# Two transposed loads in place of one for x tiles 2 and 3, and one load in place of two for the value weights

## Chip, cores, metric

One NeuronCore of a Trainium2 chip. The metric is the time of one execution on the device in microseconds (us), the median of several. The span in a profile (first to last instruction) is about 1.7 us shorter than that time. There is one core, so no die to compare with.

## The reference, cut

The result mixes two blocks over the same x of 2048 rows by 512 columns: `g * a + (1 - g) * b`, where g is a sigmoid gate of each row. Block a is linear attention with 32 heads; block b is a gated MLP.

```python
x = A_x
g = _sigmoid((x * gate_w).sum(-1, keepdims=True))
# block a
qkv = x @ wqkv                     # split into q, k, v; k and q go through w_phi and softmax
...
# block b
z = gelu(x @ w_in)
z1 = z[..., :Fh]
z2 = layernorm(z[..., Fh:])
gg = einsum('ts,bsf->btf', w_sp, z2) + b_sp
b = (z1 * gg) @ w_out
```

What matters here is the very beginning: z2 and z1 are computed for one row tile of 128 rows after another, and each needs x transposed, its half of `w_in`, and for z2 one extra column with the gate weights.

## The kernel before, the parts concerned

Tiles 0 and 1 of x are loaded plainly and transposed on TensorE; all others are transposed by their load, and the sync engine issues all of these. The loads, in the order of the program (`nc.sync` and `nc.scalar` name the engine that issues):

```python
    nc.sync.dma_start(out=xs[:, 0, :], in_=x2[0:P, :])
    nc.scalar.dma_start(out=xs[:, 1, :], in_=x2[P:2 * P, :])
    load_z2w(nc.sync, 0)
    load_z2w(nc.scalar, 1)
    load_z2w(nc.sync, 2)
    nc.scalar.dma_start(out=gaterow[0:NDT, :], in_=gate_w.rearrange("(dt p) -> dt p", p=P))
    load_z2w(nc.sync, 3)
    # ... (cut)
    def x_dma_T(i, n=1):
        nc.sync.dma_start_transpose(out=xT[:, :, i * P:(i + n) * P], in_=x2[i * P:(i + n) * P, :])

    x_dma_T(2, 2)
    for h in range(2):
        nc.sync.dma_start(
            out=w_z1[:, 2 * h:2 * h + 2, :], in_=w_in_v[:, 2 * h:2 * h + 2, 0:FH])
    for i in range(4, 8):
        x_dma_T(i)
    # ... (cut: x tiles 8 to 15, bias, folded weights)
    for h in range(2):
        nc.sync.dma_start(
            out=wv_sb[:, 2 * h:2 * h + 2, :],
            in_=A_wqkv[h * 2 * P:(h + 1) * 2 * P, 2 * D:3 * D].rearrange("(dt p) n -> p dt n", p=P),
        )
    # ... (cut: four transposed loads of w_sp)
```

TensorE works in this order (six warm-up matmuls and one short one first):

```python
        z2_first_two()          # tiles 0 and 1, by parts as the z2 weights arrive;
                                # in it, gate_T() turns the gate weights into a column of w_z2
        z2_tile(2)
        z2_tile(3)
        for c in range(NCH):
            # ... z2 of the chunk's tiles (c > 0), then z1 of its four tiles
```

Each z2 or z1 tile is eight matmuls. The first z1 tile needs the first half of the z1 weights at its first matmul, and the second half at its fifth.

The softmax here doesn't subtract the row's maximum and nothing guards it: scores larger than these inputs give would overflow.

## Time and profile before

| | before |
|---|---|
| time, median (3 runs) | 206.92 us (206.57 to 206.94) |
| span of the profiled run (a fourth run, 206.23 us) | 204.5 us |
| TensorE busy | 98% |
| z2 of tile 2 starts (first matmul) | 7.27 us |
| second z1 tile starts | 10.79 us |
| end of TensorE's work after that | 190.9 us later |

In the timeline, a row gives start, length, engine, source line, operation and count; in brackets stands how long that engine was idle before, and what ended it. PE is a matmul, PEld the load of its weights, SPq an issue on the sync engine. The landing views give kilobytes and the time from issue to landing. The lines themselves are in the prediction below. One more line of before's timeline, the five matmuls from 5.17 us in the first two tiles:

```profile
5.17 0.89 PE L191 MATMUL zp<-w_z,xT 128*128 128x344 bf16 x5
```

Five matmuls in 0.89 us: four steps of 0.145 to 0.147 us and 0.31 us for the last one.

### The profile page before, as it was taken

What the parts mean: (1) busy time and instruction counts of PE and PEld (TensorE: products, weight loads), DVE (VectorE), ACT (ScalarE), POOL (GpSimd) and SP (SyncE); (2) the same over time, 40 slices, a digit from 0 to 9 for tenths busy, and PEclk for the clock granted to TensorE, in tenths of its full rate; (3) what the DMA queues carried; (4) which work ended last, traced back from release to release, by engine and by line L of the source; (5) the groups of instructions that cost most, each with busy time, mean ns of one, the idle gap of its engine ahead of it and who ended that gap; (6) DMA issues with size and microseconds to landing.
All of it is one profiled execution on the core that took longest, in us unless ns stands there. A gap on an engine that the chain in (4) does not pass through costs nothing.

```text
span 204.5 us, 3996 instructions
## 1 busy us (share of the span) xinstructions
PE 200.6 (98%) x1557; PEld 119.5 (58%) x1557; DVE 130.5 (64%) x283; ACT 74.6 (36%) x122; POOL 45.8 (22%) x76
## 2 busy tenths in 40 slices
PE   8999999999999999999999999999999999999994
PEld 3566666655665555656565666555555555665642
DVE  4567484837977587979797788555566645633332
ACT  3466678796222333332424042222251136002303
POOL 3020202021523325334242442222204220200000
PEclk9999999999999999999999999999999999999999
DMA  5998599999997017950422229763567458552943
GB/s 188 247 209 151 117 277 209 241 194 234 207 290 168 3 38 148 317 97 15 77 47 46 51 38 114 142 126 62 108 161 79 90 112 184 61 96 51 141 80 104
DMA packets 89931, 27.22 MB, mean 133 GB/s; under 512 B 84184, under 2 KB 89912, under 8 KB 89912
## 3 DMA queue, kind: packets, MB, share of 16 engines
q1 hardware_dynamic: 87744, 24.99, 64.1%
q10 hardware_dynamic: 2168, 1.98, 3.6%
q8 instruction: 12, 0.20, 0.4%
q14 instruction: 7, 0.06, 0.1%
HBM read 4.15 MB, written 2.10 MB: 31 GB/s over the span
## 4 chain that ended last, share of the span: by engine, by line
PE 95%; DMA 2%; SPq 1%; DVE 0%; issue 0%
PE mm L454 37%; PE zp L191 17%; PE mm L355 14%; PE mm L515 8%; PE mm L509 7%; PE mm L395 7%; DMA xT<-in_A_x_dram 2%; PE kvacc L411 2%; PE at L467 2%; PE mm L520 1%; SPq L117 1%; PE zp L307 0%; PE at L478 0%; SPq L119 0%; PE pq L307 0%; DVE ob L527 0%
## 5 line engine op out<-in xcount | busy, mean ns | idle before, releaser
L454 PE MATMUL mm<-z2all,wspT 128*128 128x344 bf16 x512 | 79.9, 309 | 0.0
L454 PEld LDWEIGHTS <-wspT 128*128 128x128 bf16 x512 | 49.0, 98 | 25.3
L191 PE MATMUL zp<-w_z,xT 128*128 128x344 bf16 (+1 forms) x254 | 38.2, 309 | 0.3 <-DMA xT<-in_A_x_dram 0.3
L359 ACT ACTIVATE eq<-mm 128x512 bf16<-128x512 f32 x32 | 17.4, 594 | 51.4 <-PE mm L355 25.7
L363 DVE TENSOR_REDUCE zs<-eq 128x64 f32<-128x1024 bf16 x16 | 19.5, 1220 | 20.1 <-ACT eq L359 20.1
L191 PEld LDWEIGHTS <-xT 128*128 128x128 bf16 x254 | 24.3, 98 | 12.4 <-DMA xT<-in_A_x_dram 0.6
L359 ACT ACTIVATE ek<-mm 128x512 bf16<-128x512 f32 x32 | 17.3, 600 | 27.1 <-PE mm L355 27.1
L459 DVE SCALAR_TENSOR_TENSOR ucat<-mm,bT,z1all 128x344 bf16<-128x344 f32 x32 | 17.4, 544 | 15.1 <-PE mm L454 15.1
L372 POOL TENSOR_TENSOR eq<-eq,ratio 128x512 bf16<-128x512 bf16 x16 | 16.9, 1059 | 44.6 <-DVE ratio L371 36.6
L531 ACT ACTIVATE ob<-mm,g_inv 128x512 bf16<-128x512 f32 (+1 forms) x15 | 10.1, 680 | 33.1 <-PE mm L520 28.5
L363 DVE TENSOR_REDUCE zs<-ek 128x64 f32<-128x1024 bf16 x16 | 19.3, 1209 | 2.8 <-ACT ek L359 2.8
L515 PE MATMUL mm<-wspT,uT 128*128 128x512 bf16 (+2 forms) x85 | 20.1, 367 | 0.0
L355 PEld LDWEIGHTS <-xT 128*128 128x128 bf16 x128 | 12.2, 98 | 12.0
L372 POOL TENSOR_TENSOR ek<-ek,ratio 128x512 bf16<-128x512 bf16 x16 | 16.9, 1059 | 2.2 <-DVE ratio L371 1.7
L509 PE MATMUL mm<-wspT,oT 128*128 128x512 bf16 (+2 forms) x68 | 16.6, 366 | 0.0
L355 PE MATMUL mm<-wq_p,xT 128*128 128x512 bf16 x64 | 16.4, 379 | 0.0
L395 PE MATMUL mm<-wv_sb,xT 128*128 128x512 bf16 x64 | 16.4, 379 | 0.0
L355 PE MATMUL mm<-wk_p,xT 128*128 128x512 bf16 x64 | 16.3, 379 | 0.0
L209 DVE BATCH_NORM_STATS2 bn<-z2all 128x6 f32<-128x344 bf16 x32 | 14.9, 501 | 0.0
L206 ACT ACTIVATE z2all<-zp 128x688 bf16<-128x688 f32 x16 | 11.8, 744 | 7.6 <-PE zp L191 7.6
L260 ACT ACTIVATE z1all<-zp 128x688 bf16<-128x688 f32 x16 | 11.9, 744 | 5.1 <-PE zp L191 4.6
L515 PEld LDWEIGHTS <-uT 128*128 128x128 bf16 x85 | 8.1, 98 | 9.4 <-issue 0.2
(77 smaller groups left out, 141.8 us busy)
## 6 DMA issues: line engine op xcount, KB each, us to landing
out_dram<-ob ACTq DMA_DIRECT2D x12, 128.0 KB, 2.7
wspT<-in_B_w_out_dram SPq DMA_DIRECT2D x2, 640.0 KB, 5.5
w_z<-in_B_w_in_dram SPq DMA_DIRECT2D x2, 344.0 KB, 4.8
w_z<-in_B_w_in_dram SPq DMA_DIRECT2D x3, 172.0 KB, 3.6
wv_sb<-in_A_wqkv_dram SPq DMA_DIRECT2D x2, 256.0 KB, 4.0
wspT<-in_A_wo_dram SPq DMA_DIRECT2D x2, 256.0 KB, 4.1
out_dram<-ob SPq DMA_DIRECT2D x3, 128.0 KB, 1.8
uT<-ucat SPq DMA_TRANSPOSE x16, 2.8
```

What stands on the lines that cost most here:

```text
L191: nc.tensor.matmul(zp[:, j, 0:n], lhsT=xT[:, dt, tt * P:(tt + 1) * P], rhs=wt[:, dt, j * HF:j * HF + n], start=(dt == 0), stop=(dt == NDT ...
L209: nc.vector.bn_stats(out=bn6[:, tt, j, :], in_=z2v[:, j, :])
L260: nc.scalar.activation(out=z1all[:, tt, :].rearrange("p (j n) -> p j n", j=2), in_=zp[:, :, 0:HF], func=AF.Gelu_apprx_tanh,)
L355: nc.tensor.matmul(ps[:, :], lhsT=xT[:, dt, tt * P:(tt + 1) * P], rhs=w[:, dt, :], start=(dt == 0), stop=(dt == NDT - 1))
L359: nc.scalar.activation(out=e[:, :, a, :], in_=ps[:, :].rearrange("p (h f) -> p h f", f=DH), func=AF.Exp, scale=1.0 - 2.0 * a)
L363: nc.vector.tensor_reduce(out=z[:].rearrange("p h a -> p (h a)"), in_=e[:].rearrange("p h a f -> p (h a) f"), axis=AX.X, op=ALU.add,)
L372: nc.gpsimd.tensor_tensor(out=e[:, :, 1, :], in0=e[:, :, 1, :], in1=ratio[:, :, None].to_broadcast([P, H, DH]), op=ALU.mult)
L395: nc.tensor.matmul(v_ps[:, :], lhsT=xT[:, dt, tt * P:(tt + 1) * P], rhs=wv_sb[:, dt, :], start=(dt == 0), stop=(dt == NDT - 1))
L454: nc.tensor.matmul(gp[:, 0:HF], lhsT=wspT[:, st, tt * P:(tt + 1) * P], rhs=z2all[:, st, j * HF:(j + 1) * HF], start=(st == 0), stop=(st == ...
L459: nc.vector.scalar_tensor_tensor(out=ucat[tt % NU][:, c0 + j * HF:c0 + (j + 1) * HF], in0=gp[:, 0:HF], scalar=bT[:, tt:tt + 1], in1=z1all[ ...
L509: nc.tensor.matmul(acc, lhsT=oTs[tt][:, g, :], rhs=wo_t[:, g, c0:c1], start=start and g == 0, stop=stop and g == NG - 1)
L515: nc.tensor.matmul(acc, lhsT=uTs[tt][:, i + ft, :], rhs=w_main[i][:, ft, c0:c1], start=start and ft == 0, stop=False)
```

## The change

The intent: z2 of tile 2 needs only half of the 256 KB that it waited for. The other part keeps the number of loads as it was, so that the loads behind the value weights name the same semaphores as before.

```diff
-    x_dma_T(2, 2)
+    x_dma_T(2)
+    x_dma_T(3)
@@
-    for h in range(2):
-        nc.sync.dma_start(
-            out=wv_sb[:, 2 * h:2 * h + 2, :],
-            in_=A_wqkv[h * 2 * P:(h + 1) * 2 * P, 2 * D:3 * D].rearrange("(dt p) n -> p dt n", p=P),
-        )
+    nc.sync.dma_start(out=wv_sb[:, :, :], in_=A_wqkv[:, 2 * D:3 * D].rearrange("(dt p) n -> p dt n", p=P))
```

## The prediction

> **What bounds the kernel now.** I read the page first: shares of busy time, then the chain that ended last. Each line of the first view is an engine with its busy microseconds (share of the span).
>
> ```profile
> span 204.5 us, 3996 instructions
> PE 200.6 (98%) x1557; PEld 119.5 (58%) x1557; DVE 130.5 (64%) x283; ACT 74.6 (36%) x122; POOL 45.8 (22%) x76
> PE 95%; DMA 2%; SPq 1%; DVE 0%; issue 0%
> ```
>
> TensorE is busy for 98% of the span and holds 95% of the chain. Only some 2% of the chain is a DMA, the load of x. The same chain in order of time (start, length, what) says where that piece lies:
>
> ```profile
> 2.67 4.55 DMA xT<-in_A_x_dram
> 7.27 16.53 PE zp L191 x112
> 23.81 2.36 PE zp L191 x16
> ```
>
> So the transposed load of x tiles 2 and 3 runs from 2.67 us and is waited for until about 7.2 us; from 7.27 us on TensorE sets everything. The timeline around that point, with the issues on the sync engine (SPq), shows how much of it was really idle:
>
> ```profile
> 6.25 0.74 PE L191 MATMUL zp<-w_z,xT 128*128 128x344 bf16 x4
> 7.27 3.18 PEld L191 LDWEIGHTS <-xT 128*128 128x128 bf16 x23 [0.63 <-DMA xT<-in_A_x_dram]
> 7.27 3.54 PE L191 MATMUL zp<-w_z,xT 128*128 128x344 bf16 x23 [0.28 <-DMA xT<-in_A_x_dram]
> ```
>
> The matmul row's 0.28 us understates the stop, because the ends of pipelined matmuls are modelled. 112 matmuls in 16.53 us are 0.1476 us each. Four of them from 6.25 us would have let the fifth start at 6.25 + 4 x 0.146 = about 6.83 us; it started at 7.27. The stop is thus worth 0.44 us, and this is the whole prize. Then the issues of the loads:
>
> ```profile
> 2.67 1.45 SPq L131 DMA_TRANSPOSE xT<-in_A_x_dram  x1
> 4.17 1.08 SPq L135 DMA_DIRECT2D w_z<-in_B_w_in_dram  x2
> 5.30 5.12 SPq L131 DMA_TRANSPOSE xT<-in_A_x_dram  x4
> 23.14 1.22 SPq L152 DMA_DIRECT2D wv_sb<-in_A_wqkv_dram  x2
> 24.40 37.03 SPq L157 DMA_TRANSPOSE wspT<-in_B_w_sp_dram  x4
> ```
>
> One transpose of two tiles holds the sync engine for 1.45 us; a transpose of one tile for 5.12 / 4 = 1.28 us. The landing view for windows at those issues gives 4.6 us for the pair of tiles (2.67 + 4.6 = 7.3 us, agreeing with the end of the stop), and for the two halves of the z1 weights:
>
> ```profile
> w_z<-in_B_w_in_dram SPq DMA_DIRECT2D x1, 344.0 KB, 4.6
> w_z<-in_B_w_in_dram SPq DMA_DIRECT2D x1, 344.0 KB, 4.9
> ```
>
> The first half lands at 4.17 + 4.6 = 8.8 us, the second at about 4.8 + 4.9 = 9.7 us. Last, the DMA row of the window from 4.5 to 9.5 us in slices of 0.125 us (tenths busy; then GB/s):
>
> ```profile
> DMA  9898999995329999998969998899999999999750
> GB/s 319 286 246 248 311 281 247 199 158 94 66 37 184 287 287 333 316 270 209 220 176 341 407 330 298 330 407 385 374 363 385 352 305 319 306 272 118 84 46 18
> ```
>
> The queues are backed up through the whole window: data, not issue, sets most landings here. There is one hole, near 5.7 to 6.0 us, down to 37 GB/s, when the transposed packets meet the tail of the z2 weights.
>
> [...]
>
> **The change, part by part.** The order of instructions on the five engines is the same before and after but for two places on the sync engine: one transpose becomes two, two value-weight loads become one. The number of DMAs is unchanged. The eight DMA semaphores are handed out in turn, so every DMA between the two places takes the next semaphore in the rotation and waits for another predecessor; after the value weights the waits are the same again.
>
> 1. Tile 2 lands earlier. Half of the packets, same place in the queue. At the rate around the hole (roughly 280 GB/s after it), 128 KB less is 0.47 us: 7.23 - 0.47 = about 6.75 us. TensorE is free for it at 6.83. Its wait of 0.44 us goes, or nearly: I take 0.35 to 0.44 us.
> 2. Tile 3 must land before 6.83 + 8 x 0.147 = 8.0 us. Its issue starts at 2.67 + 1.28 + 0.04 = 4.0 us (its new semaphore wait is for x tile 0, landed at 0.81 + 2.7 = 3.5 us, so it costs nothing). Its data move where they moved before: 7.2 to 7.4 us. Slack 0.6 us.
> 3. The z1 weights are issued 2 x 1.28 - 1.45 + 0.04 = about 1.1 us later: 5.3 and 5.8 us in place of 4.17 and 4.7. TensorE, running 0.44 us earlier, loads the first z1 tile at 6.83 + 16 x 0.147 = 9.2 us and needs the second half four matmuls later, at 9.77. Before, the halves landed at 8.8 and 9.7. The first load of the kernel took about 1.3 us from issue to first moved data, so the first half can start moving at 6.6; the ring before it drains at about 6.5. Issue therefore delays it by 0.1 us at most, and the second half not at all. But the second has a slack of only 0.04 us: whatever delay is passed on becomes a stop. I take 0.1 us off.
> 4. Everything behind is issued 1.1 us later: x tile 4 lands at 10.4 + up to 1.1 and is first needed at 14.3 (16 + 32 matmuls after 7.27); the first of the folded weights lands by 20 and is needed at 26.1; the bias is needed at 23.5 and lands at 18.4. No cost.
> 5. The value weights: one issue instead of two saves perhaps 0.4 to 0.6 us of the sync engine; they land near 28 us and are first read at 45.6. The w_sp slab after them is issued about 0.6 us later than before, lands at 36.6 + 0.6, and is first read at 46.5. No cost and no gain.
>
> Sum: -0.4 + 0.1 = -0.3 us, carried to the end because TensorE has hardly a stop after 7.27 us. 206.92 - 0.3 = 206.6 us.
>
> **The rivals.** A: *the z1 weights take the place of the wait.* If the issue delay of 1.1 us passes to their landing (10.8 us against 9.77), TensorE stops 1.0 us there and the sum is +0.6 us: 207.5. For it: 0.04 us of slack. Against: the backed-up queue. B: *tile 2 lands no earlier.* [...] if both tiles' packets were already fetched, and the two counts come together at 7.2, the gain is nil: 206.9. Against it: moved data after the hole still take 0.5 us. C: *full gain*, the z1 weights landing in time: 206.5. D: a fixed cost for each transposed DMA shifts tile 3 and everything behind by some tenths: tile 3 has slack, the z1 weights have none, so 207.0.
>
> **Range and chances.** A to D span 206.5 to 207.5 and my choice lies near C and the middle. The three runs before spread over 0.37 us (206.57 to 206.94), as much as the effect. I take 206.1 to 207.3. Two per cent is 4.1 us: nine times the only stop that the change can remove, and four times its greatest delay. Faster by over 2%: 0.005. Slower by over 2%: 0.01 (only a new serialisation that the trace doesn't show). Same: 0.985.
>
> **What would show it right or wrong.** Step 1: the chain's first DMA piece ends near 6.8 us and the idle time at L191 on the x load falls to under 0.1 us. Step 3: a new idle time of TensorE on the z1 weights near 9.8 us of at most 0.2 us; 1 us there would be rival A. If the weight load for tile 2 still starts at 7.2 us, rival B. Steps 4 and 5: no new idle time of TensorE after 14 us, and the value weights' readers first starting earlier by as much as the start of the chain did. The prediction fails outright if the span moves by more than 1 us, which would have to come from a later stage that the shifted issues reorder.

Before's trace shows this: tile 2's weight load, idle for 0.63 us, started at 7.27 us, just after the one landing of the pair at 7.23; from the matmul before the stop, at 6.68 us, to the first of tile 2 it was 0.59 us, where 0.146 is usual; the pair's issue took 1.45 us, its landing came 4.6 us after the start of the issue; the smallest loads of w_phi (2 KB) landed a median 1.8 us after theirs. And of the hole: between 5.5 and 6.0 us 148 packets moved, 142 of them under 512 bytes, at a mean of 89 GB/s, and the last of the z2 weights landed at 6.2 us; a second low stretch, of 18 GB/s near 9.4 us, lies behind the z1 weights. What causes either was not tested.

## The result, and the profile after

| | before | after |
|---|---|---|
| median, 6 runs each | 206.66 us (206.34 to 206.94) | 206.13 us (205.91 to 206.91) |
| ratio, 95% interval | | 0.9979 (0.9959 to 0.9998) |

A ratio is the mean time of one kernel's runs over that of the other's runs of the same rounds, so it is not quite the ratio of the medians. The interval lies just below 1; the median lies at the low edge of the predicted range (206.1).

The profile of after puzzles at first. It is of the run that took 206.91 us, the slowest of the six; before's was of one that took 206.23 us, faster than all six of before in the table. From the page: the span is longer than in before's profile, and the load has left the chain.

```profile
span 205.2 us, 3978 instructions
PE 98%; issue 0%; DVE 0%
```

The landing view, for windows around the issues of tile 2, tile 3 and the two halves of the z1 weights:

```profile
xT<-in_A_x_dram SPq DMA_TRANSPOSE x1, 3.7
...
xT<-in_A_x_dram SPq DMA_TRANSPOSE x1, 3.0
...
w_z<-in_B_w_in_dram SPq DMA_DIRECT2D x1, 344.0 KB, 3.6
...
w_z<-in_B_w_in_dram SPq DMA_DIRECT2D x1, 344.0 KB, 4.0
```

The sync engine's issues in the timeline of after:

```profile
2.67 2.59 SPq L131 DMA_TRANSPOSE xT<-in_A_x_dram  x2
5.30 1.09 SPq L136 DMA_DIRECT2D w_z<-in_B_w_in_dram  x2
6.44 5.13 SPq L131 DMA_TRANSPOSE xT<-in_A_x_dram  x4
11.61 5.56 SPq L141 DMA_TRANSPOSE xT<-in_A_x_dram  x2
...
25.38 0.58 SPq L152 DMA_DIRECT2D wv_sb<-in_A_wqkv_dram  x1
26.01 10.57 SPq L154 DMA_TRANSPOSE wspT<-in_B_w_sp_dram  x1
```

The z1 weights are issued at 5.30 us in place of 4.17, and everything behind them later. Adding up: tile 2 lands at 2.67 + 3.7 = 6.4 us (the pair: 7.2), tile 3 at 4.0 + 3.0 = 7.0, the z1 weights at 5.3 + 3.6 = 8.9 and 5.9 + 4.0 = 9.9 us (before: 8.8 and 9.7). And yet TensorE started tile 2 later, and without waiting for x:

```profile
5.60 1.24 PEld L188 LDWEIGHTS <-xT 128*128 128x128 bf16 x5
5.88 1.31 PE L188 MATMUL zp<-w_z,xT 128*128 128x344 bf16 x5
...
7.35 8.74 PEld L188 LDWEIGHTS <-xT 128*128 128x128 bf16 x61
7.38 8.92 PE L188 MATMUL zp<-w_z,xT 128*128 128x344 bf16 x60
```

The last row runs through tiles 2, 3 and the z1 tiles without an idle mark; the first four of its matmuls finish tiles 0 and 1, so tile 2 starts at 7.38 + 4 x 0.146 = 7.96 us. The row before it tells why: five matmuls take 1.31 us where before's took 0.89. Their starts lie 0.287 us apart until about 6.8 us and 0.146 us apart from then on. In before's profile the same step from half to full rate fell before 4 us. The clock record in the packed traces agrees: full clock from 3.76 us on in before and from 6.72 us on in after. The warm-up matmuls of 512 columns, all ahead of the step, are 0.427 us apart in both; the transposes of 128 columns are 0.107 us apart in after, and 0.056 in before from 3.8 us on. In the ten profiles with nearly this start (before, after, and e1 to e4 and e9 to e12 below) this clock step falls between about 3.8 and 6.7 us; what sets the moment is not shown.

So the two profiles differ in two things, and only one is the change. After the start, nothing differs: in all ten profiles with the normal start (before, after, and e1 to e4 and e9 to e12 below), TensorE's last matmul ends 190.9 us after the second z1 tile starts, and span less start of the second z1 tile is 193.7 to 193.9 us. **The span is the start of the second z1 tile plus a constant.** Everything that follows is about what sets that start.

### The profile page after: what moved, and what is told of

Its sections match the earlier page's. It is cut to its first block, busy times and chain, and to the rows that moved or that the text cites. A ratio compares the mean times of both kernels' runs of the same rounds, so it can differ in the third digit from the quotient of the medians. Undisturbed runs are those within 1.5% of the kernel's fastest.

```text
span 205.2 us, 3978 instructions
## 1 busy us (share of the span) xinstructions
PE 200.6 (98%) x1539; PEld 120.2 (59%) x1557; DVE 130.4 (64%) x283; ACT 74.7 (36%) x122; POOL 45.7 (22%) x76
## 4 chain that ended last, share of the span: by engine, by line
PE 98%; issue 0%; DVE 0%
PE mm L451 36%; PE zp L188 19%; PE mm L352 13%; PE mm L512 8%; PE mm L392 7%; PE mm L506 7%; PE kvacc L408 2%; PE at L464 2%; PE zp L219 1%; PE mm L517 1%; PE zp L304 0%; PE pq L277 0%; PE zp L227 0%; PE at L475 0%; PE pq L304 0%
## 5 line engine op out<-in xcount | busy, mean ns | idle before, releaser
L188 PE MATMUL zp<-w_z,xT 128*128 128x344 bf16 (+1 forms) x254 | 38.8, 313 | 0.0
L369 POOL TENSOR_TENSOR eq<-eq,ratio 128x512 bf16<-128x512 bf16 x16 | 16.9, 1056 | 44.6 <-DVE ratio L368 36.6
L506 PE MATMUL mm<-wspT,oT 128*128 128x512 bf16 (+2 forms) x61 | 15.6, 365 | 0.4
L206 DVE BATCH_NORM_STATS2 bn<-z2all 128x6 f32<-128x344 bf16 x32 | 14.9, 502 | 0.0
```

What stands on the lines that cost most here:

```text
L188: nc.tensor.matmul(zp[:, j, 0:n], lhsT=xT[:, dt, tt * P:(tt + 1) * P], rhs=wt[:, dt, j * HF:j * HF + n], start=(dt == 0), stop=(dt == NDT ...
L206: nc.vector.bn_stats(out=bn6[:, tt, j, :], in_=z2v[:, j, :])
L369: nc.gpsimd.tensor_tensor(out=e[:, :, 1, :], in0=e[:, :, 1, :], in1=ratio[:, :, None].to_broadcast([P, H, DH]), op=ALU.mult)
L506: nc.tensor.matmul(acc, lhsT=oTs[tt][:, g, :], rhs=wo_t[:, g, c0:c1], start=start and g == 0, stop=stop and g == NG - 1)
```

## The experiments

"Ready" below is when TensorE has finished tiles 0 and 1 and could start tile 2; a stop is the time from there to its start. "Needed" is when TensorE came, or would have come without a stop at this very point, to the fifth matmul of the first z1 tile. All times are from the profiles, in us; the last column is the span.

| profile | x load | tile 2 landed | ready | stop | z1 weights, 2nd half landed | needed | span |
|---|---|---|---|---|---|---|---|
| before | pair | 7.23 | 6.83 | 0.44 | 9.73 | 10.21 | 204.5 |
| e2_before_again | pair | 7.30 | 7.55 | 0 | 9.70 | 10.48 | 204.8 |
| e4_wv_one_only | pair | 7.17 | 8.24 | 0 | 9.77 | 11.16 | 205.6 |
| after | split | 6.42 | 7.96 | 0 | 9.95 | 10.88 | 205.2 |
| e1_after_again | split | 6.58 | 7.25 | 0 | 10.12 | 10.17 | 204.5 |
| e3_x_split_only | split | 6.68 | 7.80 | 0 | 9.97 | 10.72 | 205.2 |
| e11_x4_ahead | split, z1 weights later | 6.45 | 7.43 | 0 | 10.99 | 10.59 | 205.4 |
| e12_gate_later | split, gate later | 6.25 | 7.12 | 0 | 10.06 | 10.04 | 204.4 |

Theory 1: the change takes away the stop for the x load, as far as TensorE is ready before it, and gives back what the later z1 weights cost. Theory 2: the 0.2% is spread from run to run, or comes from the value weights.

### The parts by themselves (five rounds, one chip)

**e1_after_again**: the changed kernel, no edit.

> The changed kernel, nothing altered, for a second profile and a tighter ratio. Theory 1 (the wait for x tiles 2 and 3 was removed; how much of it shows depends on when TensorE's clock goes from half to full rate in that execution): ratio to before 0.997 to 0.999; if its profile has the early step (matmuls 0.145 us apart by 4.5 us), the first matmul of tile 2 starts at 6.8 to 6.9 us and the span is 204.1 to 204.3 us; if it has the late step (near 6.8 us), tile 2 starts at 7.4 to 7.6 us without a wait and the span is 205.0 to 205.3. Theory 2 (the 0.2% is run-to-run spread): ratio 1.000 within 0.001, as in the control run of the kernel before.

Measured: 206.15 us (206.06 to 206.82), ratio 0.9991 (0.9976 to 1.0007). The profile has an early clock step, but tile 2 started at 7.25, not 6.8 to 6.9, and the span was 204.5, not up to 204.3. The row with the reason:

```profile
5.11 0.10 PEld L287 LDWEIGHTS <-gaterow 128*128 128x128 bf16 x1 [0.48 <-DMA gaterow<-in_gate_w_dram]
```

TensorE waited 0.48 us for the little load of the gate weights, in the middle of the first two tiles. So there is a second thing beside the clock that makes TensorE ready later than in before's profile, and it has nothing to do with the change.

**e2_before_again**: the kernel before against itself, no edit.

> Control: the kernel before against itself. Both theories: ratio 1.000, interval within 0.0015 either side. It gives a second profile of before: Theory 1 says that with the early step tile 2 starts at 7.2 to 7.3 us after a stop for the x load and the span is 204.4 to 204.6; with the late step it starts at 7.4 to 7.6 without a stop, and the span is 205.0 to 205.3, no different from the changed kernel's.

Measured: 206.49 us (206.02 to 206.85), ratio 0.9998 (0.9981 to 1.0016). The clock step came at about 5.7 us, between the two cases foreseen; tile 2 started when TensorE was ready, at 7.55 us, 0.25 us after the pair had landed. The stop of 0.44 us that the prediction took from before's one profile was not there in this execution. The interval is as wide as the effect that we look for.

**e3_x_split_only**: only the first part of the change.

```diff
-    x_dma_T(2, 2)
+    x_dma_T(2)
+    x_dma_T(3)
```

> Only the x load is split; the value weights stay two loads. Theory 1: the whole gain, ratio 0.997 to 0.999. Theory 2, or a gain from the value weights: 1.000.

Measured: 206.85 us (206.31 to 206.9), ratio 1.0014 (0.9999 to 1.0029): a miss, and on the wrong side. Its instructions and loads up to the value weights are those of after. Its profile has a late clock step (about 6.5 us), tile 2 landed at 6.68 and TensorE was ready only at 7.80; from the second z1 tile on it took the same 190.9 us as all others, so the one load more, which shifts the rotation of the semaphores, cost nothing there. In four of its six runs the mean granted clock was 0.998; it was below 1 in one of e1's six and in three of the eleven of before. That fits six executions with more late steps than usual, but the mean clock is not a sure mark of it (a later profile with a step near 6.7 us has 1.000), and six runs do not show it. It stays open.

**e4_wv_one_only**: only the second part of the change, the value weights in one load (the diff above, second hunk).

> Only the value weights are merged; the x load stays one. Theory 1: ratio 1.000, tile 2 starts as in before, the value weights' issue takes 0.6 us in place of 1.22 and nothing on TensorE moves. A gain from the value weights would show as 0.998.

Measured: 206.33 us (206.0 to 207.27), ratio 1.0003 (0.9983 to 1.0023), as expected. Its profiled run was its slowest, 207.27 us, and shows what a bad start does: a clock step near 6.5 us and

```profile
5.71 0.10 PEld L286 LDWEIGHTS <-gaterow 128*128 128x128 bf16 x1 [0.77 <-DMA gaterow<-in_gate_w_dram]
```

TensorE was ready at 8.24 us, and the x load at 7.17 didn't matter. The value weights are first read beyond 45 us; nothing there waits for them.

The four together: the control can't resolve anything below some 0.15%, and the readiness of TensorE, 6.8 to 8.2 us in six profiles, moves the span by more than the change can.

### An attempt to take the clock out (five rounds, one chip): failed

To have the clock step over before the first useful matmul, 24 tiny loads were put ahead of all others, and the warm-up lengthened:

```diff
+    pad = early.tile([P, 24, DH], BF16, name="pad")
+    for i in range(24):
+        (nc.sync, nc.scalar)[i % 2].dma_start(out=pad[:, i, :], in_=x2[0:P, i * DH:(i + 1) * DH])
     nc.sync.dma_start(out=xs[:, 0, :], in_=x2[0:P, :])
@@
-        warm_up(6)
+        warm_up(19)
```

**e5_before_late** (on before) and **e6_after_late** (on after).

> The kernel before, with 24 tiny loads (12 on each issuing queue) put ahead of its first loads, and 19 warm-up matmuls in place of 6: all loads start about 5 us later, and TensorE's clock has stepped up before the first useful matmul in every execution. Both theories: about 5 us slower than before (ratio 1.022 to 1.028). Theory 1: with the clock out of the way, the stop for the x load shows in its profile (0.3 to 0.5 us at tile 2), and the spread of its runs shrinks to about 0.3 us. Theory 2 (there is no stop worth speaking of): no such stop.

> The changed kernel with the same late start. Theory 1 (gain from the earlier landing of tile 2, capped by the z1 weights): no stop at tile 2, a stop of 0.15 to 0.35 us at the first z1 tile for the second half of its weights, and 0.1 to 0.3 us less than e5_before_late. Theory 1b (nothing caps it): no stop at the z1 weights, 0.4 to 0.5 us less. Theory 2: equal within 0.05 us.

Measured: 214.31 us (212.55 to 215.7) and 213.14 us (212.73 to 214.53), ratios 1.0392 and 1.0341. The spread became two to three times as wide, not narrower. The list of waits for e5 (us in total, times, longest):

```profile
PEld L283 <- DMA xs<-in_A_x_dram: 3.9, 2, 3.1
...
PEld L293 <- DMA gaterow<-in_gate_w_dram: 0.8, 1, 0.8
```

The warm-up did bring the step (its weight loads are 0.43 us apart up to 3.4 us and 0.21 from 3.7 us on). It ended at 6.5 us, and TensorE's matmuls then paused for 2.8 us until x tile 0 came (its weight loads, listed here, for 3.1). In this profile transposes were again 0.106 us apart from 10.4 us on, and matmuls 0.287 us apart until 13.8 us, so the half clock came back (mean granted clock 0.991). In e6 the gate weights were waited for 1.4 us. No stop for x tile 2 showed in either, as TensorE was ready at 14.9 and 14.1 us and tile 2 had landed at 13.1 and 12.7; nor did e6 stop for the z1 weights, whose second half landed at 16.3 us and was needed at 17.0. Both expectations of stops failed. The 1.2 us between the medians is therefore not the effect of the change, and the pair decides nothing about it.

**e7_z1w_act_late**: as e6, the first half of the z1 weights issued on the scalar engine's queue.

```diff
     for h in range(2):
-        nc.sync.dma_start(
+        (nc.scalar if h == 0 else nc.sync).dma_start(
             out=w_z1[:, 2 * h:2 * h + 2, :], in_=w_in_v[:, 2 * h:2 * h + 2, 0:FH])
```

> As e6_after_late, but the first half of the z1 weights is issued on the scalar engine's queue, some 0.9 us earlier, so that the sync engine's second transpose no longer delays it. Theory 1 (the cap is the issue of the z1 weights): the z1 stop shrinks below 0.1 us, 0.1 to 0.3 us less than e6_after_late. Rival (the cap is the data rate): the weights now compete with the transposes, tile 2 or 3 lands later by as much, no gain or up to 0.4 us more.

Measured: 214.56 us (213.16 to 216.07), ratio 1.0393. In its list of waits:

```profile
PEld L191 <- DMA xT<-in_A_x_dram: 2.3, 2, 1.5
```

Tile 2 landed 4.9 us after its issue (3.6 in e6) and tile 3 6.1 us after (2.9 in e6), and TensorE stopped for both. Its 95% interval (1.0355 to 1.0431) lies mostly, but not wholly, above e6's (1.0316 to 1.0367), so the time alone doesn't settle it; the landings speak for the rival in the expectation: with the first half of the weights issued on the other queue, tile 2 came 1.3 us and tile 3 3.2 us later after its issue than in e6.

**e8_x4_ahead_late**: as e6, with x tile 4 loaded ahead of the z1 weights (the diff is under e11).

> As e6_after_late, but x tile 4 is loaded before the z1 weights: the suspected cost of the later issue doubled, 1.28 us more of issue and 128 KB more of data ahead of the z1 weights. Theory 1 (no slack is left at the z1 weights): their stop grows to 0.7 to 1.4 us, 0.5 to 1.1 us more than e6_after_late. Theory 1b (slack is left): less than 0.2 us more.

Measured: 214.55 us (214.06 to 215.05, four runs), ratio 1.0399. The second half of the z1 weights landed at 17.9 us (e6: 16.3), but TensorE, after 1.7 us of wait for the gate weights and a fresh half-clock stretch (mean granted clock 0.992), needed it only at 18.2 us: no stop at the z1 weights. The 1.4 us between the medians of e8 and e6 cannot be put down to them.

### Making the load bind, in place of the clock (five rounds, one chip)

Since TensorE's readiness can't be fixed, the loads were moved to where they come later than it in every execution.

**e9_pair_after_z1w** and **e10_split_after_z1w**: before and after, each with its x load(s) issued behind the z1 weights. For e9:

```diff
-    x_dma_T(2, 2)
     for h in range(2):
         nc.sync.dma_start(
             out=w_z1[:, 2 * h:2 * h + 2, :], in_=w_in_v[:, 2 * h:2 * h + 2, 0:FH])
+    x_dma_T(2, 2)
```

> The kernel before with its one load of x tiles 2 and 3 issued after the z1 weights. Its data now come 700 KB later in the queue, so that it lands later than TensorE is ready in every execution (at 6.8 to 8.2 us in the profiles so far). Theory 1 (whatever tile 2 waits for sets the end, one for one): it lands at 8.7 to 9.3 us, tile 2 starts with it, the first z1 tile doesn't wait, the span is the start of the second z1 tile plus 193.8 us = 206.0 to 206.6, time 207.7 to 208.3, and the spread of runs shrinks below 0.5 us since the clock's step no longer matters.

> The changed kernel (two loads, value weights in one) with both loads issued after the z1 weights: the change by itself where TensorE always waits for x. Theory 1: tile 2 lands 0.5 to 0.7 us before the pair of e9_pair_after_z1w does, tile 3 at about the pair's time, no other stop, and the time is 0.4 to 0.7 us less than that of e9_pair_after_z1w, clear of its spread. Rival B of the prediction (both tiles land together): equal within 0.1 us.

Measured: e9 208.05 us (207.95 to 208.38), ratio 1.0081 (1.0067 to 1.0094); e10 207.58 us (207.26 to 208.44), ratio 1.0063 (1.0044 to 1.0081). The weight loads of tile 2 in the timelines of e9 and then of e10:

```profile
9.43 4.64 PEld L191 LDWEIGHTS <-xT 128*128 128x128 bf16 x33 [1.92 <-DMA xT<-in_A_x_dram]
```

```profile
9.00 5.08 PEld L188 LDWEIGHTS <-xT 128*128 128x128 bf16 x36 [1.27 <-DMA xT<-in_A_x_dram]
```

Now TensorE waits for x in both. The pair landed at 9.38 us, the single tile 2 at 8.96; tile 2 started 0.42 us earlier, and the profiled spans differ by 0.4 us (206.7 and 206.3). The load was issued 0.23 us earlier in e10 (3.91 us, against 4.14), but that isn't the cause: the second half of the z1 weights, ahead of it in the queue, landed at 8.39 us in e9 and at 8.38 in e10, and after that the pair took 0.99 us, the single tile 0.58. The medians differ by 0.47 us, the means by 0.36. Tile 3 landed at 9.54 us, and was needed at 9.01 + 1.17 = 10.2. This is the mechanism of the change by itself, one for one; the landing gained a little less than the 0.5 to 0.7 us expected. One run of e10 took 208.44 us, as long as the slowest of e9; why is not known, and with it the two 95% intervals overlap, so the difference is not clear of the spread as was expected; the landings and the two profiles carry the verdict, not the times alone. The spread of e9, 0.43 us, is less than half of that of before in the same rounds (1.03), as expected where the clock's step no longer counts; that of e10, 1.18 us, did not shrink.

**e11_x4_ahead**: the changed kernel with x tile 4 loaded ahead of the z1 weights, to double the suspected give-back.

```diff
+    x_dma_T(4)
     for h in range(2):
         nc.sync.dma_start(
             out=w_z1[:, 2 * h:2 * h + 2, :], in_=w_in_v[:, 2 * h:2 * h + 2, 0:FH])
-    for i in range(4, 8):
+    for i in range(5, 8):
         x_dma_T(i)
```

> The changed kernel with x tile 4 loaded before the z1 weights: their later issue, the suspected give-back, doubled. Theory 1 (the z1 weights have next to no slack): second half lands at 10.9 to 11.6 us, TensorE stops in the first z1 tile, time 206.7 to 207.5. Rival (plenty of slack): time as e1_after_again, 206.2 within 0.2.

Measured: 207.14 us (207.06 to 207.22), ratio 1.0035 (1.0021 to 1.0049). The first z1 tile in its timeline:

```profile
10.01 0.55 PEld L189 LDWEIGHTS <-xT 128*128 128x128 bf16 x5 [0.43 <-DMA w_z<-in_B_w_in_dram]
11.03 3.22 PE L189 MATMUL zp<-w_z,xT 128*128 128x344 bf16 x21 [0.26 <-DMA w_z<-in_B_w_in_dram]
```

The halves landed at 9.96 and 10.99 us and TensorE stopped at each; the steps to these two matmuls are 0.388 and 0.570 us in place of 0.146, so 0.24 + 0.42 = 0.67 us lost. Delaying the z1 weights by one issue and 128 KB cost the median about 1 us against e1's 206.15 (on another chip): they had next to no slack. And all six runs lie within 0.16 us, as expected if the clock's step is hidden where a load binds every time.

**e12_gate_later**: a candidate for a better version. The transpose of the gate weights moves three matmuls later on TensorE, and the gate column of the second quarter is taken afterwards.

```diff
         z_part(0, 0, HF, True)
-        gate_T()
         one(0, 1, 0)
         one(1, 0, 0)
         z_part(1, 0, HF, True)
         one(1, 1, 0)
+        gate_T()
         for tt in range(2):
-            one(tt, 1, 1)
+            z_part(tt, 0, HF, False, dt=1)
@@
-            z_part(tt, HF, HF + 1, False)
+            for dt in range(2):
+                z_part(tt, HF, HF + 1, False, dt=dt)
```

> A candidate for a better version: the changed kernel, with the transpose of the gate weights moved three matmuls later on TensorE, because two of six profiles show TensorE stopped 0.5 and 0.8 us for their load. Costs two matmuls of one column, 0.06 us. If that stop matters: no stop on the gate weights, median 205.9 to 206.15, and fewer runs above 206.3. If the z1 weights set the floor all the same, or the clock's step does: as e1_after_again, 206.2 within 0.15.

Measured: 206.2 us (206.0 to 206.57), ratio 0.999 (0.9976 to 1.0004). There was no stop for the gate weights and TensorE was ready at 7.12 us with a clock step at about 5 us, but the time is that of e1. The profile shows what came in its place, in the first z1 tile:

```profile
9.60 1.10 PE L188 MATMUL zp<-w_z,xT 128*128 128x344 bf16 x6
```

Six matmuls with five steps: 1.10 - 0.31 = 0.79 us, where 5 x 0.146 would be 0.73. The step to the fifth matmul of the first z1 tile was 0.208 us; it started at 10.10 us, and the second half of the z1 weights had landed at 10.06. That is the give-back, seen directly: as soon as TensorE is a little early, the z1 weights stop it. No version here is shown to be better than after.

## Why the prediction was right

The range and the class were right; two of its terms were mis-sized, both so that the gain looked larger than the traces support. That the measured gain came out above the prediction all the same is put down to luck below, which no run shows.

**Step 1, tile 2 lands earlier: right in kind, and the load was freer than predicted.** 6.75 us was predicted; five profiles of the split in its place show 6.25 to 6.68, against 7.17 to 7.30 for the pair. Rival B (both land together) falls. But the prize was mis-sized: "0.35 to 0.44 us" was read off one profile in which TensorE happened to be ready early. That profile is of a run of 206.23 us, and its stop was taken off a median of 206.92 us. In two further profiles with the pair there was no stop at all, because the clock step or the gate weights had made TensorE late. The 0.44 us is a best case, not the typical one.

**Step 2, tile 3: right.** 6.8 to 7.3 us, always before it was needed. Its issue waits for the semaphore of x tile 1 (landed at 3.65 us in after), not of tile 0, which is as harmless. Rival D (a fixed cost of each transposed load) was not tested by itself; in e10 tile 3 landed 0.16 us after e9's pair.

**Step 3, the z1 weights: right that they take part of the gain back, too small.** The second half landed at 9.95 to 10.12 us against 9.70 to 9.77 before, so 0.2 to 0.4 us later, where 0.1 was allowed ("the second half not at all"). With TensorE ready at 6.83 us it would be needed at 9.77 us: an estimate from these rows is a stop of 0.2 to 0.35 us, so a net gain of only 0.1 to 0.25 in the best case. e12 shows such a stop (0.06 us, at a readiness of 7.12), e11 what more delay costs. Rival A is thus partly true, with 0.2 to 0.4 of the issue delay of 1.1 us passed on, not all of it; and rival C (full gain) falls.

The step that failed is "data, not issue, sets most landings", and with it "issue therefore delays it by 0.1 us at most". The DMA row of after, in the same window and slices as before's in the prediction, shows what came in its place:

```profile
GB/s 341 341 402 372 348 292 280 238 179 111 133 188 276 258 154 45 55 77 44 132 22 55 154 253 220 286 352 407 374 363 385 374 396 396 376 366 381 321 290 238
```

Between 6.25 and 7.25 us (slices 15 to 22) before moved 176 to 341 GB/s, after only 22 to 154: the packets of the x tiles were all but through, and those of the z1 weights, issued 1.1 us later, came thinly. This holds for each of the seven profiles: a mean of 269 to 293 GB/s in that stretch in the three with the pair, 44 to 103 in the four with the split in its place and nothing else moved ahead of the z1 weights. In e11, where the z1 weights are issued 1.3 us later still (6.62 us), the low stretch lies between 7.25 and 8.6 us, at 0 to 121 GB/s. So the queue did not stay backed up; the later issue left a hole in it. (The 1.3 us that the prediction took from issue to first moved data is about 1.0 us in before's trace, where the first load is issued at 0.81 us and data move from 1.83 us; the hole doesn't depend on it.)

**Step 4, no cost behind: right, with wrong sizes.** "Up to 1.1" us was too little: the weights for k that are folded landed at 22.6 us in after's profile (19.9 before), the last load of w_phi at 24.6 (23.0). They were needed at 26.8 us. The two long x transposes took 5.56 us to issue in place of 4.20; why is not explored.

**Step 5, the value weights: right.** One issue of 0.58 us in place of 1.22; the first w_sp slab landed at 39.1 us (36.6 before) and is read from 46 us on. e4's ratio is 1.000 within 0.002.

**The sum.** -0.3 us was predicted, from 206.92 to 206.6 us; 206.13 was measured, and 0.26 of the 0.5 us between is only the base, as six runs of before gave 206.66. The comparisons on a shared set of rounds give 0.9979 and 0.9991, which are -0.4 and -0.2 us. By the estimate under step 3 the change can give at most some 0.25 us, and nothing where TensorE is late, so a mean gain of 0.4 us is more than the mechanism explains; the rest would be the luck of the starts in six runs, which is not shown. The split without the value weights gives +0.3 us, with an interval that just includes 1. Over all undisturbed runs, the mean of 45 of before is 206.44 us and that of 12 of after 206.23; but the fastest are 205.86 and 205.91, so the best case doesn't seem to have moved, though 45 runs against 12 give before more chances of a low one. Shown is the mechanism (e9 against e10, the landings, e11, e12); the average gain in the kernel as it is, between nothing and 0.4 us, is not settled. Two comparisons of three with the predicted sign are not enough to call the size right.

## What to carry to other kernels

Before you size a stop at the very start of a kernel, take several profiles: the moment of TensorE's clock step and the landing of the smallest load move TensorE's readiness by more than a tenth of the first ten microseconds (here from 6.83 to 8.24 us, with the step between 3.8 and 6.7 us and stops of up to 0.77 us for the gate weights). When a load is split so that its first part lands earlier, list what is issued behind it and how much slack the next one has; here the gain ended at the second half of the z1 weights, whose landing at 10.06 us held up e12 by 0.06 us. Look at the DMA rate for a hole behind the split load: here it was 22 to 154 GB/s where before moved 176 to 341, and the z1 weights, issued 1.1 us later, landed 0.2 to 0.4 us later. To test a small wait, move it to where it binds in every execution: in two of three such kernels here the spread of runs fell from about 1 us to 0.2 and 0.4; in the third it stayed.
